# Infini-attention and SwiGLU layers on one core: the memory update's products in four column tiles of two heads, with the instruction order chosen anew

## Chip, cores and metric

The kernel runs on one core of one Trainium2 chip. The metric is the time of one execution in device microseconds, as the median of repeated executions. Five engines work side by side and wait for each other by semaphores: TensorE (PE, with its weight loads shown apart as PEld), VectorE (DVE), ScalarE (ACT), GpSimd (POOL) and SyncE (SP), which issues most DMAs.

## What is computed

The input is one sequence of 2048 tokens with 512 features. Two layers are applied, each an attention block A and a feed-forward block B, each on a layer norm of its input and added back to it. The two layers use the same weights.

```python
def _A_ref(x, wq, wk, wv, wo, beta):       # H = 32 heads of Dh = 16, N = 4 segments of L = 512
    ...                                    # q, k, v: [B, H, N, L, Dh]
    phi = lambda t: jnp.where(t > 0, t + 1.0, jnp.exp(t))
    g = _sigmoid(beta).reshape(1, H, 1, 1)
    for s in range(N):
        logits = einsum('bhqd,bhkd->bhqk', qs, ks) * scale + mask      # causal within the segment
        a_dot = einsum('bhqk,bhkd->bhqd', softmax(logits), vs)
        pq = phi(qs)
        num = einsum('bhld,bhde->bhle', pq, M)
        den = einsum('bhld,bhd->bhl', pq, z)[..., None] + 1e-06
        outs.append(g * (num / den) + (1.0 - g) * a_dot)
        pk = phi(ks)
        M = M + einsum('bhld,bhle->bhde', pk, vs)                      # the memory update
        z = z + einsum('bhld->bhd', pk)
    return o @ wo

def _B_ref(x, w1, w3, w2):                  # 512 -> 1376 -> 512
    return (silu(x @ w1) * (x @ w3)) @ w2
```

Each head keeps a memory M of 16 x 16 and a vector z of 16, which carry from one segment to the next. Only the sums over earlier segments are read, so the update is done after the first three segments of each layer, six times in all.

## The kernel before

The work is cut into eight blocks (two layers of four segments, `g` from 0 to 7). Heads lie in four groups `G` of eight, so that one group's 8 x 16 features fill the 128 partitions.

Per block, `project` makes q and k (features on partitions) and `va` (tokens on partitions, V with a column of ones behind each head's 16, which gives z and the softmax sums along with the products). `attention` goes through 20 units. Each unit has score matmuls (`lg`, line 952, names `R...`), which use row tiles of 32 partitions for four heads at a time; an exp on ScalarE over up to 2048 columns (line 961); and masks on GpSimd (line 974). The four PSUM banks for scores hold one full unit, so a unit's scores wait for the exp of the unit before. In block 0 the units are split in halves. After each group's units follow the products with V (`attend`, line 1003, names `C...`), which use column tiles of 32 columns, their eviction, a DMA transpose (line 1013), the division (`normalise`, lines 1028 to 1041) and another transpose (line 1044). Then come `out_proj`, a layer norm with transposes (lines 692 to 728), and `ffn`, whose g and u matmuls go through a tanh on ScalarE (line 1118) and two multiplications on VectorE (lines 1120 and 1124). The matmuls of projections, feed-forward and the memory all go through the helpers `whole` and `quarters`, so their lines are 388 and 393.

The memory update (`memory_update`): `phi` makes pk from k (exp `px` at line 812, then lines 814 and 816), a DMA transpose (line 825) turns it to tokens on partitions, and for each half `hf` of the groups one call of the op `dacc` multiplies it with `va`. A call makes, for each of two groups and four token tiles, one matmul with 128 weight columns (the group's features) and 136 moving columns (8 heads x 17). Only the 8 diagonal blocks of 16 x 17 of each product are wanted, the other heads' blocks are computed beside them. VectorE adds the product to the sum `macc` (line 844, 272 columns), and multiplies the sum with the 0/1 pattern `bdm` into `mb` (line 846), which clears the unwanted blocks. In the next block `memory_read` multiplies pq with `mb`: `mden` (8 columns, the denominators) and four `mnum` (128 columns), and VectorE divides (`om`, line 882).

The order of all instructions on each engine is chosen when the kernel is built: the class `Sched` places ops one by one by estimated durations, with priorities. `SLACK`, `LOOK`, `C_AGE` and `MARGIN` shape how it picks; `PRIO`, `GATE` and `FINE` shift single groups of ops, by block. An op has a mode: `R` for row tiles, `C` for column tiles, `F` otherwise. Matmuls that may be done either way (`flex`) stand, per pass between two score units, all as four column tiles (`quarters`) when the pass holds an op of mode `C` and all others are flexible, and whole otherwise:

```python
split = any(x.mode == "C" for x in run) and all(x.mode == "C" or x.flex for x in run)
for x in run:
    x.wide = not split
```

An op of mode `C` that became ready less than `C_AGE` ago is put behind all others while the pass is not one of column tiles. `hand_over` adds waits of GpSimd for some ops of VectorE in the first 70 us of the plan.

Of the kernel before, what the change touches and what calls it, by code (L numbers as in the profile page):

```python
# [4 lines left out]
ALU = mybir.AluOpType  # L5
BF16 = mybir.dt.bfloat16
F32 = mybir.dt.float32

P = 128
# [3 lines left out]
NCG = 4  # L13
# [4 lines left out]
LT = 4  # L18
# [18 lines left out]
MARGIN = {"": 300.0, "bnag": 500.0, "bnst": 200.0, "d": 200.0, "dacc": 300.0, "evk": 500.0, "evq": 50.0, "evv": 300.0, "gpr": 800.0, "hmr": 200.0, "lnrs": 200.0, "lnve": 100.0, "macc": 100.0, "mden": 100.0, "mnum": 500.0, "mrec": 1200.0, "norm": 300.0, "oT": 1200.0, "oadd": 100.0, "ph": 500.0, "phexp": 200.0, "phmin": 300.0, "pkT": 3000.0, "q": 200.0, "r": 100.0, "resA": 100.0, "resB": 500.0, "t": 2000.0, "tanh": 50.0}  # L37


class Pool:  # L40
# [373 lines left out]
def o_pe(ns):  # L414
# [4 lines left out]


PRIO = {
    ("bnst", 1): -51.1, ("bnst", 2): 1000, ("d", 0): 301.1, ("evX", 0): 1329.07, ("evk", 2): 1000, ("evv", 1): 599.1,
    ("g", 2): 6366.8, ("g", 4): 6907.74, ("g", 5): 990, ("gp", 0): -603.05, ("gpr", 1): 300, ("k", 2): 49.98,
    ("k", 3): 652.13, ("k", 4): -4638.56, ("k", 6): -2000.08, ("km", 0): 1000, ("mblk", 0): 1000,
    ("mden", 3): 2359.82, ("mrec", 2): -996.7, ("norm", 6): 999.95, ("o", 5): 2080.58, ("phexp", 3): -939.7,
    ("phmin", 1): -9.95, ("phmin", 2): -1651.05, ("phmin", 6): -337.3, ("q", 1): -2343.51, ("q", 6): -4830.46,
    ("r", 5): -1301, ("rdg", 6): 300, ("tanhr", 1): 300, ("u", 0): 394.62, ("u", 6): -310.2, ("v", 1): 40.3,
    ("v", 3): -1300.1,
}
GATE = {  # L430
    ("bnst", 2): -76, ("bnst", 3): 2, ("bnst", 4): -1, ("bnst", 5): 2, ("km", 3): 19, ("km", 4): 16, ("km", 7): 14,
    ("ph", 0): -38, ("phexp", 0): -10, ("q", 1): 3, ("q", 2): 5, ("v", 1): -211, ("v", 2): -2, ("v", 4): 1,
    ("v", 6): 5, ("v", 7): 10,
}
FINE = {
    ("", 0, 8): 1000, ("bnag", 4, 5): 50, ("d0", 4, 6): 1001, ("d1", 3, 1): 1, ("d1", 5, 3): 1351, ("d1", 5, 6): 1299,
    ("d2", 3, 0): 50, ("d3", 1, 6): 0.1, ("d3", 2, 2): 43.3, ("d3", 2, 5): 1.25, ("evX", 0, 2): -1000,
    ("evX", 2, 3): -1000, ("evX", 2, 7): -1000, ("evX", 3, 6): 3, ("evv", 1, 1): 2050, ("exp", 3, 0): 0.05,
# [5 lines left out]
    ("lnve", 1, 0): -1003, ("macc", 5, 1): -50, ("mask", 0, 1): -990, ("mask", 0, 14): -3700, ("mask", 0, 18): -3,  # L444
    ("mask", 5, 20): -301, ("mnum", 1, 2): -0.95, ("mnum", 5, 3): -10, ("mrec", 6, 0): -47, ("norm", 1, 1): -326.19,
    ("norm", 1, 2): -1111.33, ("norm", 1, 3): -902.53, ("norm", 2, 6): -997, ("norm", 3, 3): -10,
    ("norm", 4, 3): -1050, ("norm", 5, 1): 950, ("norm", 6, 7): -3, ("o0", 6, 0): 300.1, ("o0", 7, 0): 300,
# [8 lines left out]
}  # L456


def build(nc, A_x, A_wq, A_wk, A_wv, A_wo, A_beta, B_w1, B_w3, B_w2, out):
# [9 lines left out]
    def sb(name, shape, dt=BF16):  # L469
        return nc.alloc_sbuf_tensor(name, shape, dt)  # L470
# [351 lines left out]
    def memory_update(g, z, pkb):  # L822
        kt = new("W")
        for hf in range(2):
            dmaT(lambda e, hf=hf: e.dma_start_transpose(
                pkt_r[kt.slot][:, 2 * hf:2 * hf + 2, :, :].rearrange("p g i c -> p (g i) c"),
                pk_r[pkb.slot][:, 2 * hf:2 * hf + 2, :].rearrange("p g n -> p (g n)")),
                 reads=[(pkb, hf)], writes=[(kt, hf)], bufs=[pkb, kt], prio=g + 0.1, name="pkT")
        mb = new("mb")
        for hf in range(2):  # L830
            B = new("B")

            def fn(e, mm, hf=hf, B=B):
# [10 lines left out]
            dve(lambda e, B=B, mv=mv: e.tensor_tensor(mv, bank(B)[:, 0:272], mv, ALU.add), 272, True,  # L844
                reads=[(B, 0), ("macc", hf)], writes=[("macc", hf)], bufs=[B], prio=g - 95.0, name="macc")
            dve(lambda e, hf=hf: e.tensor_tensor(mb_r[mb.slot][:, 2 * hf:2 * hf + 2, :, :].rearrange("p a h d -> p a (h d)"),
                                                 macc[:, 2 * hf:2 * hf + 2, :, :].rearrange("p a h d -> p a (h d)"),
                                                 bdm[:].rearrange("p h d -> p (h d)")[:, None, :].to_broadcast([P, 2, 136]), ALU.mult),
                375, reads=[("macc", hf), "bdm"], writes=[(mb, hf)], bufs=[mb], prio=g - 300, name="mblk")
        mstate["mb"] = mb  # L850

# [77 lines left out]
    def attention(s, g, z, oms, parts):  # L929
        z.ot = new("W")  # L930
        cnt = 0
        for pi, part in enumerate(parts):
# [219 lines left out]
    for layer in range(2):  # L1152
        for s in range(NS):
# [8 lines left out]
                gth_op = gate_constants()  # L1162
            z = project(s, g, X, g == 0)
            if s == 0 and layer == 1:
                pool(lambda e: e.memset(macc[:], 0.0), 544, writes=[("macc", 0), ("macc", 1)], prio=g)
            oms = None
            if s > 0:
                pqb = new("W")
# [61 lines left out]
```

## Time and profile before

| | |
|---|---|
| time, median of 3 runs | 486.26 us (486.24 to 486.32) |
| span of the profiled execution | 483.3 us |
| time outside the span, by the median | 2.96 us |
| TensorE, matmuls busy | 469.3 us |
| VectorE busy | 392.0 us |
| ScalarE busy | 392.4 us |
| GpSimd busy | 244.7 us |
| matmuls of `dacc` | 88 whole, 32 in column tiles recorded |

The profile's page names no separate time for the profiled execution. Its span, from the first to the last instruction, stands for it, and the rest to the median lies around it. Busy matmul time includes the latency of each matmul at its end, so a TensorE that is shown as busy may still have room; steps from one start to the next are more reliable. A row of grouped instructions shows line, engine, operation, out<-in, shapes and count, then busy time and mean duration, then the idle time just before them and what ended it. A few per cent of the matmul records can be missing.

### The profile page before, as it was taken

What the parts mean: (1) busy time and instruction counts of PE and PEld (TensorE: products, weight loads), DVE (VectorE), ACT (ScalarE), POOL (GpSimd) and SP (SyncE); (2) the same over time, 40 slices, a digit from 0 to 9 for tenths busy, and PEclk for the clock granted to TensorE, in tenths of its full rate; (3) what the DMA queues carried; (4) which work ended last, traced back from release to release, by engine and by line L of the source; (5) the groups of instructions that cost most, each with busy time, mean ns of one, the idle gap of its engine ahead of it and who ended that gap; (6) DMA issues with size and microseconds to landing.
All of it is one profiled execution on the core that took longest, in us unless ns stands there. A gap on an engine that the chain in (4) does not pass through costs nothing.

```text
span 483.3 us, 13285 instructions
## 1 busy us (share of the span) xinstructions
PE 469.3 (97%) x5619; PEld 223.5 (46%) x5654; DVE 392.0 (81%) x814; ACT 392.4 (81%) x356; POOL 244.7 (51%) x380
## 2 busy tenths in 40 slices
PE   7989999999999999999999999999999999999997
PEld 4543446754444444444444444544444434455544
DVE  5999899988988888779986789876996697578572
ACT  2999999989989987899989999889998799730230
POOL 4777455853546545656565556665473464510000
PEclk9999999999999999999999999999999999999999
DMA  7778367342235622451462324524064322320401
GB/s 257 260 131 147 72 123 88 63 72 55 23 77 84 91 41 41 71 92 37 66 99 56 67 44 78 88 58 63 3 100 72 61 56 56 73 50 14 90 3 45
DMA packets 106522, 37.07 MB, mean 77 GB/s; under 512 B 99200, under 2 KB 104448, under 8 KB 106464
## 3 DMA queue, kind: packets, MB, share of 16 engines
q1 hardware_dynamic: 104016, 31.41, 35.0%
q0 software_dynamic: 1488, 4.03, 4.3%
q8 instruction: 44, 0.72, 0.6%
q10 hardware_dynamic: 960, 0.79, 0.5%
q14 instruction: 14, 0.11, 0.1%
HBM read 8.43 MB, written 2.10 MB: 22 GB/s over the span
## 4 chain that ended last, share of the span: by engine, by line
PE 81%; DVE 7%; ACT 5%; issue 4%; DMA 2%; POOL 0%; SPq 0%; POOLq 0%
PE psall L388 49%; PE psall L393 12%; PE psall L952 11%; PE psall L1003 7%; ACT e L961 3%; DVE W L551 2%; DMA W<-W 1%; DMA W<-xn 1%; PE psall L581 1%; DVE W L816 1%; ACT px L812 1%; DVE xn L710 1%; DVE xs L551 1%; ACT th L1118 0%; DVE x_tok L1056 0%
## 5 line engine op out<-in xcount | busy, mean ns | idle before, releaser
L961 ACT ACTIVATE e<-psall 128x2048 bf16<-128x2048 f32 (+1 forms) x180 | 301.3, 1700 | 29.3 <-PE psall L952 27.6
L974 POOL TENSOR_SCALAR_AFFINE_SELECT e<-e 128x512 bf16<-128x512 bf16 x256 | 164.2, 660 | 164.5 <-ACT e L961 156.9
L388 PE MATMUL psall<-W,w 128*128 128x512 bf16 (+1 forms) x521 | 110.0, 350 | 0.0
L388 PEld LDWEIGHTS psall<-W,w 128*128 128x128 bf16 x521 | 47.0, 98 | 44.9 <-issue 8.1
L1120 DVE SCALAR_TENSOR_TENSOR gp<-th,psall 128x512 bf16<-128x512 bf16 x80 | 53.7, 679 | 15.1 <-ACT th L1118 14.9
L1118 ACT ACTIVATE th<-psall 128x512 bf16<-128x512 f32 x80 | 47.2, 602 | 18.8 <-PE psall L393 17.5
L1124 DVE SCALAR_TENSOR_TENSOR h<-gp,psall 128x512 bf16<-128x512 bf16 x80 | 54.2, 679 | 8.1 <-PE psall L388 7.4
L388 PE MATMUL psall<-w,h 128*128 128x512 bf16 (+1 forms) x218 | 53.8, 380 | 1.4 <-issue 1.0
L393 PE MATMUL psall<-W,w 128*32 128x512 bf16 (+1 forms) x796 | 44.5, 371 | 0.0
L692 DVE BATCH_NORM_STATS2 ln<-x_tok 128x6 f32<-128x512 bf16 x64 | 42.3, 681 | 0.3
L1003 PE MATMUL psall<-e,va 128*32 128x256 bf16 (+3 forms) x1088 | 41.4, 292 | 1.2 <-POOL e L974 1.2
L952 PE MATMUL psall<-W 16*128 16x256 bf16 (+3 forms) x544 | 41.4, 294 | 0.5 <-ACT e L961 0.3
L952 PE MATMUL psall<-W,km 32*128 32x256 bf16 (+3 forms) x544 | 40.8, 291 | 0.3
L551 DVE CAST W<-psall 128x512 bf16<-128x512 f32 x46 | 31.0, 681 | 8.4 <-PE psall L388 7.9
L1143 DVE TENSOR_TENSOR x_tok<-psall,x_tok 128x512 bf16<-128x512 f32 (+1 forms) x33 | 22.1, 670 | 19.4 <-PE psall L393 10.7
L388 PE MATMUL psall<-W,wk 128*128 128x512 bf16 (+1 forms) x137 | 32.9, 356 | 0.7 <-DVE W L551 0.5
L551 DVE CAST xs<-psall 128x512 bf16<-128x512 f32 x38 | 25.6, 682 | 9.6 <-PE psall L1003 9.4
L1003 PEld LDWEIGHTS psall<-e,va 128*32 128x32 bf16 x1088 | 24.6, 96 | 18.0 <-issue 2.8
L388 PEld LDWEIGHTS psall<-w,h 128*128 128x128 bf16 (+1 forms) x233 | 20.9, 98 | 25.9 <-issue 4.8
L952 PEld LDWEIGHTS psall<-W 16*128 16x128 bf16 x544 | 13.1, 91 | 42.0 <-ACT e L961 39.1
L710 DVE TENSOR_SCALAR xn<-x_tok,ln 128x512 bf16<-128x512 bf16 x64 | 29.5, 504 | 3.6 <-POOL ln L701 3.5
L1036 POOL TENSOR_TENSOR og<-xg,rd 128x256 bf16<-128x256 bf16 (+1 forms) x45 | 25.5, 584 | 10.2 <-DVE rd L1030 8.2
(87 smaller groups left out, 589.0 us busy)
## 6 DMA issues: line engine op xcount, KB each, us to landing
w<-in_B_w_dram SPq DMA_DIRECT2D x4, 688.0 KB, 8.1
out_dram<-x_tok SPq DMA_DIRECT2D x15, 128.0 KB, 1.7
km<-W POOLq DMA_DIRECT2D x24, 64.0 KB, 2.7
w<-in_B_w_dram POOLq DMA_DIRECT2D x3, 384.0 KB, 4.1
x_tok<-in_A_x_dram POOLq DMA_DIRECT2D x2, 512.0 KB, 4.7
xg<-xs SPq DMA_TRANSPOSE x36, 3.1
W<-og SPq DMA_TRANSPOSE x36, 2.4
wk<-in_A_wk_dram SPq DMA_DIRECT2D x1, 512.0 KB, 4.4
```

Of the source, the lines that this page charges most:

```text
L388: return e.matmul(out, lhsT, rhs, **k)
L393: o = e.matmul(out[c:c + 32], lhsT[:, c:c + 32], rhs, tile_position=(0, c), **k)
L551: return e.tensor_copy(dst(), src())
L692: dve(lambda e: e.bn_stats(ln_r[st.slot][:, i, 0:6], x_tok[:, tt, :]), 540, reads=[("x", tt)], writes=[(st, 0, i)], bufs=[st], prio=prio, ...
L710: op = S.add([o_dve(512, False, 1.45)], lambda e, i=i, k=k, tt=tt, xn=xn: e.tensor_scalar(xn_r[xn.slot][:, k, :], x_tok[:, tt, :], ln_r[st ...
L952: o = e.matmul(S4[:, sps(pg), c:c + n], kk[32 * pg:32 * pg + r, G, 128 * j:128 * j + 128], q_r[z.q.slot][32 * pg:32 * pg + r, G, 128 * t1 ...
L961: act(lambda e, N=N, ebuf=ebuf, pgs=pgs, sps=sps: e.activation(e_r[ebuf.slot][:, pgs[0]:pgs[-1] + 1, 0:N], S4[:, sps(pgs[0]):sps(pgs[-1]) ...
L974: pool(lambda e, ebuf=ebuf, c=c: e.affine_select(e_r[ebuf.slot][:, :, c:c + 128], e_r[ebuf.slot][:, :, c:c + 128], pattern=[[0, 4], [1, 128]],
L1003: o = e.matmul(bank(X)[32 * pg:32 * pg + 32, base + W - n:base + W], va_r[z.va.slot][:, j, h:h + 32], e_r[eb.slot][:, pg, c:c + n], start= ...
L1118: act(lambda e, NW=NW, B=B, th=th: e.activation(th_r[th.slot][:, 0:NW], bank(B)[:, 0:NW], ACT.Tanh, scale=0.5), NW, reads=[(B, 0)], writes ...
L1120: dve(lambda e, NW=NW, B=B, th=th, gp=gp: e.scalar_tensor_tensor(gp_r[gp.slot][:, 0:NW], th_r[th.slot][:, 0:NW], 1.0, bank(B)[:, 0:NW], AL ...
L1124: dve(lambda e, NW=NW, B=B, gp=gps[fg], h=hs[fg]: e.scalar_tensor_tensor(h_r[h.slot][:, 0:NW], gp_r[gp.slot][:, 0:NW], 0.5, bank(B)[:, 0:N ...
```

## The change

A call of `dacc` makes four matmuls where it made one: each takes 32 weight columns (two heads' features), goes to a column tile of its own, and has as moving columns only those two heads' 34. The sum `macc` keeps 34 columns for each group and not 136: per 32 partitions the two heads' blocks of 17. The multiplication into `mb` reads these 34 columns four times over, once for each place, times the pattern, and still writes all 136 columns of a group. The op is given mode `C` and stands no longer among the flexible ones. All constants of the order are new.

```diff
-SLACK = {"pe": 30.0, "act": 60.0, "dve": 60.0, "pool": 0.0, "sp": 30.0}
-LOOK = {"pe": 90.0, "act": 10.0, "dve": 10.0, "pool": 5.0, "sp": 200.0}
-C_AGE = 3000.0
+SLACK = {"pe": 37.0, "act": 72.0, "dve": 89.0, "pool": 112.0, "sp": 27.0}
+LOOK = {"pe": 91.0, "act": 30.0, "dve": 20.0, "pool": 80.0, "sp": 302.0}
+C_AGE = 6933.0
...
 PRIO = {
...
 GATE = {
...
 FINE = {
...
-    macc = sb("macc", [P, NCG, 8, 17], F32)
+    macc = sb("macc", [P, NCG, 34], F32)
...
-    pool(lambda e: e.memset(macc[:], 0.0), 544, writes=[("macc", 0), ("macc", 1)], prio=CP + 3)
+    pool(lambda e: e.memset(macc[:], 0.0), 136, writes=[("macc", 0), ("macc", 1)], prio=CP + 3)
...
-            def fn(e, mm, hf=hf, B=B):
+            def fn(e, hf=hf, B=B):
                 o = None
                 for a in range(2):
                     G = 2 * hf + a
                     for i in range(LT):
-                        o = mm(e, bank(B)[:, 136 * a:136 * a + 136], pkt_r[kt.slot][:, G, i, :],
-                                     vheads(va_r[z.va.slot], i, 8 * G, 8)[:, :, 0:17], start=(i == 0), stop=(i == LT - 1))
+                        for c in range(4):
+                            o = e.matmul(bank(B)[32 * c:32 * c + 32, 34 * a:34 * a + 34], pkt_r[kt.slot][:, G, i, 32 * c:32 * c + 32],
+                                         vheads(va_r[z.va.slot], i, 8 * G + 2 * c, 2)[:, :, 0:17], start=(i == 0), stop=(i == LT - 1),
+                                         tile_position=(0, 32 * c))
                 return o
-            pe(fn, 8 * 65, reads=[(kt, hf)] + [(z.va, i) for i in range(LT)], writes=[(B, 0)],
+            pe(fn, 8 * 30, mode="C", reads=[(kt, hf)] + [(z.va, i) for i in range(LT)], writes=[(B, 0)],
                bufs=[B, kt, z.va], hold=[mb], prio=g + 0.3 - 900, name="dacc")
-            mv = macc[:, 2 * hf:2 * hf + 2, :, :].rearrange("p a h d -> p (a h d)")
-            dve(lambda e, B=B, mv=mv: e.tensor_tensor(mv, bank(B)[:, 0:272], mv, ALU.add), 272, True,
+            mv = macc[:, 2 * hf:2 * hf + 2, :].rearrange("p a h -> p (a h)")
+            dve(lambda e, B=B, mv=mv: e.tensor_tensor(mv, bank(B)[:, 0:68], mv, ALU.add), 68, True,
                 reads=[(B, 0), ("macc", hf)], writes=[("macc", hf)], bufs=[B], prio=g - 95.0, name="macc")
-            dve(lambda e, hf=hf: e.tensor_tensor(mb_r[mb.slot][:, 2 * hf:2 * hf + 2, :, :].rearrange("p a h d -> p a (h d)"),
-                                                 macc[:, 2 * hf:2 * hf + 2, :, :].rearrange("p a h d -> p a (h d)"),
-                                                 bdm[:].rearrange("p h d -> p (h d)")[:, None, :].to_broadcast([P, 2, 136]), ALU.mult),
+            dve(lambda e, hf=hf: e.tensor_tensor(mb_r[mb.slot][:, 2 * hf:2 * hf + 2, :, :].rearrange("p a (c h) d -> p a c (h d)", h=2),
+                                                 macc[:, 2 * hf:2 * hf + 2, :][:, :, None, :].to_broadcast([P, 2, 4, 34]),
+                                                 bdm[:].rearrange("p (c h) d -> p c (h d)", h=2)[:, None, :, :].to_broadcast([P, 2, 4, 34]), ALU.mult),
                 375, reads=[("macc", hf), "bdm"], writes=[(mb, hf)], bufs=[mb], prio=g - 300, name="mblk")
...
-    SPLIT = (0,)
+    SPLIT = 20
...
-                groups = [(0, 1), (2, 3)] if g in SPLIT else [(0, 1, 2, 3)]
+                groups = [(0, 1), (2, 3)] if g == 0 and cnt < SPLIT else [(0, 1, 2, 3)]
```

`PRIO`, `GATE`, `FINE` and `MARGIN` have other entries throughout, and the memset of `macc` between the layers shrinks as the first one does. Counted in the built order, `dacc` has twelve calls of 32 matmuls where it had eleven of 8 and one of 32; score units come in 179 passes where there were 178; and 28 evictions of `va` stand on VectorE and 4 on ScalarE, where there were 23 and 9.

More of the change, by code (lines that the diff above doesn't have):

```diff
@@ L33 @@
 R_SLACK = 0.0
-SLACK = {"pe": 30.0, "act": 60.0, "dve": 60.0, "pool": 0.0, "sp": 30.0}
-LOOK = {"pe": 90.0, "act": 10.0, "dve": 10.0, "pool": 5.0, "sp": 200.0}
-C_AGE = 3000.0
-MARGIN = {"": 300.0, "bnag": 500.0, "bnst": 200.0, "d": 200.0, "dacc": 300.0, "evk": 500.0, "evq": 50.0, "evv": 300.0, "gpr": 800.0, "hmr": 200.0, "lnrs": 200.0, "lnve": 100.0, "macc": 100.0, "mden": 100.0, "mnum": 500.0, "mrec": 1200.0, "norm": 300.0, "oT": 1200.0, "oadd": 100.0, "ph": 500.0, "phexp": 200.0, "phmin": 300.0, "pkT": 3000.0, "q": 200.0, "r": 100.0, "resA": 100.0, "resB": 500.0, "t": 2000.0, "tanh": 50.0}
+SLACK = {"pe": 37.0, "act": 72.0, "dve": 89.0, "pool": 112.0, "sp": 27.0}
+LOOK = {"pe": 91.0, "act": 30.0, "dve": 20.0, "pool": 80.0, "sp": 302.0}
+C_AGE = 6933.0
+MARGIN = {"": 50.0, "XT": 1200.0, "bnag": 500.0, "bnst": 100.0, "d": 200.0, "dacc": 300.0, "evX": 100.0, "evk": 500.0, "evq": 100.0, "evv": 300.0, "exp": 50.0, "g": 50.0, "gpr": 200.0, "hT": 100.0, "hmr": 500.0, "k": 50.0, "ldbeta": 500.0, "ldw": 500.0, "ldwk": 50.0, "ldwo": 3000.0, "ldwq": 300.0, "ldwv": 800.0, "ldx": 50.0, "lnrs": 800.0, "lnve": 300.0, "macc": 50.0, "mask": 50.0, "mblk": 500.0, "mde": 200.0, "mden": 200.0, "mnum": 500.0, "mrec": 1200.0, "norm": 300.0, "oT": 3000.0, "oadd": 500.0, "om": 50.0, "ph": 500.0, "phexp": 200.0, "phmin": 300.0, "pkT": 3000.0, "q": 200.0, "r": 300.0, "resA": 100.0, "resB": 500.0, "stx": 300.0, "t": 2000.0, "tanh": 50.0, "u": 50.0, "warm": 100.0, "xT": 800.0, "xt": 200.0}
 class Pool:
@@ L421 @@
 PRIO = {
[L422 to L426, printed above, removed]
@@ L427 @@
-    ("r", 5): -1301, ("rdg", 6): 300, ("tanhr", 1): 300, ("u", 0): 394.62, ("u", 6): -310.2, ("v", 1): 40.3,
-    ("v", 3): -1300.1,
+    ("bnag", 2): 598.5, ("bnag", 3): 1321.3, ("bnag", 4): -3404.9, ("bnag", 5): -2272, ("bnst", 3): 125.9, ("d", 1):
+    3258.4, ("d", 3): 2319.2, ("evk", 3): 1034.2, ("evq", 2): 2243.6, ("evv", 1): 463.6, ("evv", 2): -181.7, ("exp",
+    5): -133.8, ("g", 2): 8591.1, ("g", 4): 9710.64, ("gp", 2): -2081.1, ("hmr", 7): 1313.8, ("k", 2): 36.38, ("k",
+    4): -5667.56, ("k", 6): -5229.18, ("km", 1): 3839.8, ("lnrs", 5): 1479, ("lnve", 0): 1277, ("lnve", 4): -692.5,
@@ new lines @@
+    ("mask", 2): 135.9, ("mask", 3): 356.6, ("mden", 3): 1473.72, ("mden", 6): -676.3, ("mnum", 3): 406.9, ("mnum",
+    6): -5341.9, ("mrec", 3): -474, ("norm", 5): 2198.8, ("o", 4): -1099.5, ("o", 5): 2352.98, ("ph", 0): -122.8,
+    ("ph", 1): -2832.4, ("phexp", 0): -3794.5, ("phexp", 3): -3111.5, ("phexp", 5): 3154.1, ("phmin", 2): -6822.85,
+    ("phmin", 3): -1266.3, ("phmin", 6): 3338.8, ("q", 1): -1403.51, ("q", 6): -8143.16, ("r", 1): -122.2, ("r", 5):
+    -3416.4, ("rd", 2): 13.4, ("rdg", 5): 657.7, ("t", 2): 1662.4, ("u", 0): -161.4, ("u", 2): -0.8, ("u", 3):
@@ L429 @@
+    -1109, ("u", 4): -2518.4, ("v", 3): -2015.7,
 }
 GATE = {
-    ("bnst", 2): -76, ("bnst", 3): 2, ("bnst", 4): -1, ("bnst", 5): 2, ("km", 3): 19, ("km", 4): 16, ("km", 7): 14,
-    ("ph", 0): -38, ("phexp", 0): -10, ("q", 1): 3, ("q", 2): 5, ("v", 1): -211, ("v", 2): -2, ("v", 4): 1,
-    ("v", 6): 5, ("v", 7): 10,
+    ("bnst", 2): -1, ("bnst", 3): 3, ("bnst", 4): -3, ("k", 4): -17, ("km", 3): 16, ("km", 4): 17, ("km", 7): 17,
+    ("ph", 0): -101, ("phexp", 0): -24, ("q", 1): 4, ("v", 1): -201, ("v", 3): 1, ("v", 4): 2, ("v", 6): 10, ("v",
@@ L434 @@
+    7): 4,
 }
 FINE = {
-    ("", 0, 8): 1000, ("bnag", 4, 5): 50, ("d0", 4, 6): 1001, ("d1", 3, 1): 1, ("d1", 5, 3): 1351, ("d1", 5, 6): 1299,
-    ("d2", 3, 0): 50, ("d3", 1, 6): 0.1, ("d3", 2, 2): 43.3, ("d3", 2, 5): 1.25, ("evX", 0, 2): -1000,
-    ("evX", 2, 3): -1000, ("evX", 2, 7): -1000, ("evX", 3, 6): 3, ("evv", 1, 1): 2050, ("exp", 3, 0): 0.05,
[5 rows of a table removed]
-    ("lnve", 1, 0): -1003, ("macc", 5, 1): -50, ("mask", 0, 1): -990, ("mask", 0, 14): -3700, ("mask", 0, 18): -3,
-    ("mask", 5, 20): -301, ("mnum", 1, 2): -0.95, ("mnum", 5, 3): -10, ("mrec", 6, 0): -47, ("norm", 1, 1): -326.19,
@@ L1164, in build @@
             if s == 0 and layer == 1:
-                pool(lambda e: e.memset(macc[:], 0.0), 544, writes=[("macc", 0), ("macc", 1)], prio=g)
+                pool(lambda e: e.memset(macc[:], 0.0), 136, writes=[("macc", 0), ("macc", 1)], prio=g)
             oms = None
```

3 lines of the change are left out of this document (1 added, 2 removed), and 24 rows, old and new, of the table FINE.

## The prediction

> **What bounds the kernel now.** I read the page first: the busy shares and the chain that ended last.
>
> ```profile
> span 483.3 us, 13285 instructions
> PE 469.3 (97%) x5619; PEld 223.5 (46%) x5654; DVE 392.0 (81%) x814; ACT 392.4 (81%) x356; POOL 244.7 (51%) x380
> PE 81%; DVE 7%; ACT 5%; issue 4%; DMA 2%; POOL 0%; SPq 0%; POOLq 0%
> ```
>
> TensorE is busy nearly throughout and carries 81% of the chain. But a busy matmul row contains pipeline latency, so I asked for windows next (columns: elapsed, then busy time of PE, PEld, DVE, ACT, POOL).
>
> ```profile
> 33.00:57.00 24.00, 23.77 (x306) 10.93 (x310) 21.07 (x56) 23.98 (x30) 16.24 (x28) 1.00 0.72 116
> 57.00:82.00 25.00, 23.95 (x274) 12.62 (x269) 23.93 (x52) 24.66 (x22) 13.62 (x23) 1.00 0.62 103
> 82.00:108.50 26.50, 26.24 (x351) 16.95 (x355) 24.10 (x54) 24.39 (x22) 17.87 (x26) 1.00 0.49 74
> 108.50:419.00 310.50, 306.99 (x3176) 137.00 (x3205) 255.38 (x522) 282.13 (x237) 168.90 (x256) 1.00 0.37 64
> ```
>
> Two regimes. From 33 to 82 us ScalarE is full (23.98 of 24.00, 24.66 of 25.00): there a shorter matmul is worth nothing, a shorter ScalarE stretch everything. From 82 to 419 us TensorE is the tighter engine; between 108.5 and 419 it idles 310.50 - 306.99 = 3.5 us, and that is all that a better order could win there. The clock is 1.00 throughout.
>
> How a unit of attention works is in the timeline of PE (start, duration).
>
> ```profile
> 356.33 0.40 PE L952 MATMUL psall<-W 16*128 16x512 bf16 x4
> 356.66 2.55 PE L388 MATMUL psall<-W,w 128*128 128x512 bf16 x11
> 359.14 0.40 PE L952 MATMUL psall<-W 16*128 16x384 bf16 x8
> ```
>
> Score matmuls (L952) stand 2.81 us apart (359.14 - 356.33), with eleven 512-column matmuls between: (2.55 - 0.38) / 10 = 0.217 us each, 0.38 being the last one's own duration by the same group's mean (380 ns, quoted below). So the pass between two scores is plain work on TensorE, plus about 0.1 us at each change between score and other matmuls. Reducing work inside such passes shortens the kernel one for one, as long as ScalarE's exp, 1.88 us a unit, is ready.
>
> ```profile
> L961 ACT ACTIVATE e<-psall 128x2048 bf16<-128x2048 f32 x140 | 263.2, 1880 | 28.1 <-PE psall L952 26.4
> ```
>
> **The tail** was read separately, because work behind the last score may be only filler.
>
> ```profile
> 418.84 0.40 PE L952 MATMUL psall<-W,km 32*128 32x384 bf16 x8
> 422.63 1.26 PE L1003 MATMUL psall<-e,va 128*32 128x512 bf16 x32
> 423.72 13.34 PE L393 MATMUL psall<-W,w 128*32 128x512 bf16 x244
> 436.88 3.63 PE L393 MATMUL psall<-wo,W 128*32 128x512 bf16 x64
> 452.52 0.84 PE L393 MATMUL psall<-w,W 128*32 128x192 bf16 x32 [0.97 <-DMA W<-xn]
> 424.66 1.24 SPq L1013 DMA_TRANSPOSE xg<-xs  x1
> 432.56 1.19 SPq L1044 DMA_TRANSPOSE W<-og  x1
> 446.08 2.61 SPq L728 DMA_TRANSPOSE W<-xn  x2
> 447.43 5.05 DMA W<-xn
> 452.52 27.68 PE psall L393 x571
> ```
>
> After the last scores (418.84) come filler, the last product with V (422.63), more filler, the output projection (436.88), filler, and at 452.52 the last feed-forward, 27.68 us. That last one waited 0.97 us for the transposed `xn`. The path there is transposes and vector work (424.66, 432.56, 446.08), so the 33.68 us from 418.84 to 452.52 hang on that path, and filler removed there only becomes waiting.
>
> **The change, part by part.**
>
> *The products.* One row per form: 136 columns on the whole array, 136 columns in four column tiles (one call of before ran so already), and the denominator's 8-column matmuls as the nearest tiny ones.
>
> ```profile
> L388 PE MATMUL psall<-W,w 128*128 128x512 bf16 x376 | 91.3, 380 | 0.0
> L388 PE MATMUL psall<-va,W 128*128 128x136 bf16 x88 | 7.1, 226 | 0.4 <-DMA W<-W 0.2 <-DVE om L882 0.2
> 33.04 0.66 PE L388 MATMUL psall<-va,W 128*128 128x136 bf16 x8
> 44.17 0.66 PE L388 MATMUL psall<-va,W 128*128 128x136 bf16 x8
> 68.21 0.66 PE L388 MATMUL psall<-va,W 128*128 128x136 bf16 x8
> 71.50 0.66 PE L388 MATMUL psall<-va,W 128*128 128x136 bf16 x8 [0.20 <-DVE om L882]
> 83.40 0.66 PE L388 MATMUL psall<-va,W 128*128 128x136 bf16 x8
> 86.92 0.67 PE L393 MATMUL psall<-va,W 128*32 128x136 bf16 x32
> L388 PE MATMUL psall<-mb,W 128*128 128x8 bf16 x96 | 3.5, 176 | 0.0
> 78.44 0.58 PE L388 MATMUL psall<-mb,W 128*128 128x8 bf16 x16
> ```
>
> A whole call has step (0.66 - 0.226) / 7 = 62 ns, so it takes 8 x 62 = 0.50 us. In tiles the eight groups of four have the same step, (0.67 - 0.226) / 7 = 63 ns: four tiles stream together. With 34 columns a group streams a quarter. Bounds of its step: a quarter of 62, 15 ns, and 62, no gain at all. The nearest row for a step not set by columns is the 8-column one: (0.58 - 0.176) / 15 = 27 ns. I take 27: a call costs 0.22 us, 0.28 less (bounds 0.37 and 0). Of twelve calls, four stand early (33.04, 44.17, 68.21, 71.50), where ScalarE is full, and earn nothing. Eight earn: **-2.24 us** (bounds -3.0, 0).
>
> [...]
>
> *What waits on the products.* Counted in the two orders with the steps above, the next denominator (`mden`) stands at least 12 us of TensorE work behind the products that it reads (before: 6). The two vector steps between cost
>
> ```profile
> L844 DVE TENSOR_TENSOR macc<-psall,macc 128x272 f32<-128x272 f32 x12 | 5.1, 430 | 0.2
> L846 DVE TENSOR_TENSOR mb<-macc,bdm 128x272 bf16<-128x272 f32 x12 | 6.1, 511 | 0.1
> ```
>
> The sum shrinks from 272 to 68 columns (bounds: 0 to 0.35 us less each; I take 0.2, off the path); the spreading multiply keeps its 272 results. So that a product now waits for a column pass costs nothing: these 12 us cover it. The smaller clearing of `macc` on GpSimd is off the path as well. `SPLIT` changes nothing: all 20 units of the first block stay split.
>
> *The order, TensorE.* Counted in the two orders: before, 125 four-tile groups of 512 columns stand behind the last scores outside the projection and the last feed-forward; after, 116. Nine groups are pulled ahead: 9 x 0.217 = **+1.94 us** on the passes where TensorE bounds. The tail gains little:
>
> ```profile
> W<-og SPq DMA_TRANSPOSE x36, 2.4
> ```
>
> From the last V product to the projection stand 57 groups, 12.4 us, where before had 61, 13.2; the path between needs 11.2 to 12.4 (423.72 to a transpose issued at 432.56, with 2.4 of landing, from the issue or from its end at 433.75), so it just fits. Two more groups stand ahead of the V product. Two groups net: **-0.4 us** (bounds -1 to +0.6).
>
> *The order, ScalarE.*
>
> ```profile
> L812 ACT ACTIVATE px<-W 128x1024 bf16<-128x1024 bf16 x24 | 25.8, 1075 | 0.0
> L550 ACT ACTIVATE va<-psall 128x512 bf16<-128x512 f32 x9 | 5.4, 602 | 0.0
> ```
>
> Within the first 40 exps one `px` goes and one eviction comes: 1.08 - 0.60, **-0.47 us**, at full value. Within the next 20 stands one `px` more, +1.08; only the first half of that block is full, so **+0.5 us** (bounds 0, +1.08). Net five evictions of `va` move to VectorE, all behind that block, where both have room.
>
> *The waits.* Of the 3.5 us in which TensorE idles I take a fifth as gone, **-0.7 us**, a choice: slightly less work is asked of VectorE before the reads of `mb`. Bounds -2.5, +2.5.
>
> Sum: -2.24 + 1.94 - 0.4 - 0.47 + 0.5 - 0.7 = -1.37 us. The page gives no other time for its execution than the span, 483.3; the median of the runs is 486.26, and the 2.96 us around the span stay. So 486.26 - 1.37 = **484.9 us**. About 0.2%, 0.97 us, is what a measurement of this kernel can tell from no change.
>
> **The rivals.** *The waits go*: all the idle time that can go, -2.5 for -0.7, gives 483.1. For it: 3.5 us are there. Against: they are many small ones.
>
> *ScalarE holds the second block to its end* (108.5): the calls at 83.40 and 86.92 earn nothing either, six are left, -1.68, and `px` counts in full: -1.68 + 1.94 - 0.4 - 0.47 + 1.08 = +0.47, 486.7. For it: 24.39 of 26.50. Against: TensorE 26.24.
>
> *The calls do not get shorter* (slower): the step of a group stays near 62 ns since four weight loads and four matmuls must be handed over for it. Then the pulled work is not paid: 1.94 - 0.4 - 0.47 + 1.08 = +2.15, 488.4. Its far end is 27 ns for each matmul in series, 0.86 for 0.50 us, 8 x 0.36 more, 491.3. [...] It decides from a step of about 45 ns, where eight calls save 1.1 us. For it: no group shorter than 128 columns is in the trace in tiles. [...]
>
> That the change doesn't do what it says is out: the built order has twelve calls of 32 matmuls with 34 columns.
>
> **How the numbers follow.** Chances: the forecast 0.40, waits gone 0.13, ScalarE 0.20, calls not shorter 0.27, of which 0.05 for the far end. Faster 0.53, same 0.20, slower 0.27. The range leaves out that far end and as much of the others: from 482.4 (the waits gone and the step at 15 ns, 483.1 - 0.7) to 489.4 (488.4 and the tail at its bound). The forecast alone: 484.0 to 485.3.
>
> **What would show it.** Right: `va,W` rows of 34 columns with a call of about 0.4 us from first start to last end (0.2 and the last matmul's own 0.2), `macc` near 0.2 us, the last scores about 1 us earlier, a wait of 2 to 3 us for `xn` ahead of the last feed-forward, ScalarE as full as before to 82 us. Wrong: a call of 0.6 us or more; the last scores not earlier although the calls are short, which would mean waits of the new order; or no wait ahead of the last feed-forward, which would mean that the tail hangs on work after all.

## The result and the profile after

The changed kernel takes 483.3 us (median of 6 runs, 481.6 to 483.83), the kernel before 486.25 us beside it (6 runs). The ratio is 0.9944, with a 95% interval of 0.9927 to 0.9961: 2.7 us faster (2.95 us between the two medians), where 1.4 us were forecast. The runs of either kernel lie on two levels some 1.5 us apart, so only ratios of runs on one chip are compared below.

The page of the changed kernel (span, busy shares, chain), then its groups by shape (mean ns behind the comma).

```profile
span 479.9 us, 14227 instructions
...
PE 467.6 (97%) x6090; PEld 222.1 (46%) x6122; DVE 390.6 (81%) x816; ACT 389.9 (81%) x351; POOL 245.4 (51%) x383
...
PE 79%; ACT 13%; DVE 6%; issue 1%; DMA 1%
```

```profile
L843 DVE TENSOR_TENSOR mb<-macc,bdm 128x272 bf16<-128x272 f32 x12 | 5.9, 494 | 0.0
...
L834 PE MATMUL psall<-va,W 128*32 128x34 bf16 x384 | 4.8, 180 | 0.0
...
L841 DVE TENSOR_TENSOR macc<-psall,macc 128x68 f32<-128x68 f32 x12 | 2.7, 221 | 0.5 <-PE psall L834 0.5
```

The calls are what was forecast: 34 columns, the sum `macc` near 0.2 us, `mb` hardly shorter. The windows show ScalarE still full to 82 us, as forecast, and TensorE after it as full as before.

```profile
33.00:57.00 24.00, 23.95 (x369) 10.30 (x369) 21.02 (x58) 24.00 (x29) 12.92 (x23) 1.00 0.58 106
57.00:82.00 25.00, 23.59 (x342) 12.55 (x341) 23.10 (x50) 24.84 (x24) 16.70 (x29) 1.00 0.61 119
82.00:108.50 26.50, 26.16 (x472) 17.74 (x473) 23.92 (x54) 24.57 (x22) 17.19 (x26) 1.00 0.36 55
```

The surprise is in the tail. The timeline of PE and the last lines of the chain:

```profile
417.47 0.40 PE L949 MATMUL psall<-W,km 32*128 32x384 bf16 x8
...
421.73 1.27 PE L1000 MATMUL psall<-e,va 128*32 128x512 bf16 x32
...
435.13 3.63 PE L393 MATMUL psall<-wo,W 128*32 128x512 bf16 x64
...
448.73 0.84 PE L393 MATMUL psall<-w,W 128*32 128x192 bf16 x32 [0.36 <-DMA W<-xn]
```

```profile
445.56 3.12 DMA W<-xn
448.73 27.68 PE psall L393 x569
```

From the last scores to the last feed-forward it is 448.73 - 417.47 = 31.26 us, where before had 33.68. A wait of 2 to 3 us for `xn` was forecast there; it is 0.36 us. The landing of the last transposed `xn` took 3.12 us, before 5.05.

The whole span in stretches, from the starts in the timelines of ScalarE (first exp, 61st exp) and PE (last scores, last feed-forward), in us. Second traces of both kernels and the three experiments that matter most stand beside them. The tail goes from the last scores to the last feed-forward, the rest from there to the end. (In the last two kernels the first matmuls of the last feed-forward run on from the group ahead without a gap, in one row, and its start is taken from the single matmuls.)

| kernel | to first exp | to 61st exp | to last scores | tail | rest | span |
|---|---|---|---|---|---|---|
| before | 12.04 | 96.49 | 310.31 | 33.68 | 30.8 | 483.3 |
| before, second trace | 13.01 | 96.64 | 310.39 | 33.58 | 30.8 | 484.4 |
| after | 11.73 | 95.54 | 310.20 | 31.26 | 31.2 | 479.9 |
| after, second trace | 11.20 | 95.57 | 310.78 | 31.27 | 31.1 | 479.9 |
| new order, old products | 11.58 | 96.81 | 312.73 | 31.28 | 31.1 | 483.5 |
| old order, new products | 12.33 | 96.70 | 311.99 | 32.54 | 30.8 | 484.4 |
| the same, 30 instructions less | 11.53 | 96.79 | 309.24 | 32.54 | 30.8 | 480.9 |

### The profile page after: what moved, and what is told of

Read it like the earlier page. It is cut to its first block, busy times and chain, and to the rows that moved or that the text cites. A ratio compares the mean times of both kernels' runs of the same rounds, so it can differ in the third digit from the quotient of the medians.

```text
span 479.9 us, 14227 instructions
## 1 busy us (share of the span) xinstructions
PE 467.6 (97%) x6090; PEld 222.1 (46%) x6122; DVE 390.6 (81%) x816; ACT 389.9 (81%) x351; POOL 245.4 (51%) x383
## 4 chain that ended last, share of the span: by engine, by line
PE 79%; ACT 13%; DVE 6%; issue 1%; DMA 1%
PE psall L388 45%; PE psall L393 19%; ACT e L958 10%; PE psall L949 9%; PE psall L1000 6%; ACT px L807 1%; PE psall L576 1%; DVE x_tok L1053 1%; DMA W<-xn 1%; DVE om L879 1%; DVE W L811 1%; DVE xs L546 1%; DVE W L809 1%; PE psall L834 1%; DVE gp L1117 1%
## 5 line engine op out<-in xcount | busy, mean ns | idle before, releaser
L388 PE MATMUL psall<-W,w 128*128 128x512 bf16 (+1 forms) x494 | 103.3, 351 | 0.6 <-DVE W L546 0.3
L388 PEld LDWEIGHTS psall<-W,w 128*128 128x128 bf16 x494 | 44.9, 98 | 43.2 <-issue 7.9
L388 PE MATMUL psall<-w,h 128*128 128x512 bf16 (+1 forms) x203 | 49.1, 380 | 1.1 <-issue 0.6
L393 PE MATMUL psall<-W,w 128*32 128x512 bf16 (+1 forms) x904 | 49.9, 368 | 0.1
L546 DVE CAST W<-psall 128x512 bf16<-128x512 f32 x46 | 31.2, 681 | 5.2 <-PE psall L388 5.1
L393 PEld LDWEIGHTS psall<-W,w 128*32 128x32 bf16 x904 | 23.3, 97 | 20.5 <-issue 0.9
L388 PE MATMUL psall<-W,wk 128*128 128x512 bf16 (+1 forms) x131 | 31.7, 355 | 0.5 <-DVE W L546 0.5
L393 PE MATMUL psall<-w,h 128*32 128x512 bf16 (+3 forms) x588 | 32.0, 363 | 0.0
```

Of the source, the lines that this page charges most:

```text
L388: return e.matmul(out, lhsT, rhs, **k)
L393: o = e.matmul(out[c:c + 32], lhsT[:, c:c + 32], rhs, tile_position=(0, c), **k)
L546: return e.tensor_copy(dst(), src())
```

## Experiments: the two halves of the change

**Products alone and order alone.** The first kernel keeps the order of before op for op and takes the new products; the second keeps the new order and takes the old ones.

```diff
 first: before, with memory_update's products and macc of the change, and
-            split = any(x.mode == "C" for x in run) and all(x.mode == "C" or x.flex for x in run)
+            split = any(x.mode == "C" or x.name == "dacc" for x in run) and all(x.mode == "C" or x.flex for x in run)
 second: after, with memory_update's products and macc of before, and
-            split = any(x.mode == "C" for x in run) and all(x.mode == "C" or x.flex for x in run)
+            split = any(x.mode == "C" and x.name != "dacc" for x in run) and all(x.mode == "C" or x.flex for x in run)
```

> The kernel before, with its order of every engine kept op for op, and only the products changed: twelve calls of 32 tiled matmuls with 34 columns, the sum of 34 columns for each group; passes that hold a call go in column tiles. Theory A (the products earn where TensorE bounds, the order gives part of it back): nothing is pulled ahead here, so the last scores come some 1.9 to 2.2 us earlier than 418.84 us in the profile (eight calls of 0.28 us); the tail behind them, all filler, keeps its length or grows by what it waits; the time goes to about 484 to 484.5 us. Theory B (the gain was made by the new order alone, above all in the first block, and the products earn next to nothing): last scores at 418.4 to 419.1, time 486.3. The va,W rows read about 0.4 us a call in both.

> The changed kernel, with its order of every engine kept op for op, and only the products and the sum put back to 136 columns on the whole array (passes that were column-tiled for them alone go whole). Theory A: it loses what eight calls earned, 2.2 us: last scores at about 419.7 instead of 417.47 us, time about 485.5. Theory B: last scores stay at 417.4 to 417.8, time 483.3 to 483.7. In both, the first exp of the second block's units (the 21st) stays near 31.8 us against 33.0 before, since the first block has no memory product on its path.

Measured: products alone 485.97 us, ratio 1.0012 (1.0001 to 1.0022); order alone 485.21 us, ratio 0.9999 (0.9989 to 1.0010). Each half alone earns nothing, both together 2.7 us. Theory B falls: the order alone is not the gain. Theory A falls as well in its first half. The price of a call is not in question. Timeline of PE, new order with old products, then the changed kernel, the same place:

```profile
240.35 0.67 PE L388 MATMUL psall<-va,W 128*128 128x136 bf16 x8
240.86 1.89 PE L388 MATMUL psall<-W,w 128*128 128x512 bf16 x8
```

```profile
237.59 0.38 PE L834 MATMUL psall<-va,W 128*32 128x34 bf16 x32
237.81 1.92 PE L393 MATMUL psall<-W,w 128*32 128x512 bf16 x32
```

240.86 - 240.35 = 0.51 us for a call before, 0.22 now. So with the old order the saving must have turned into waits, and its timeline shows two that before does not have. Products alone, then before at the same two places:

```profile
157.74 1.46 PE L388 MATMUL psall<-W,wk 128*128 128x512 bf16 x6 [1.22 <-DVE h L1126]
...
363.63 0.51 PE L393 MATMUL psall<-w,W 128*32 128x192 bf16 x16 [0.94 <-DVE gp L1095]
```

```profile
155.87 1.46 PE L388 MATMUL psall<-W,wk 128*128 128x512 bf16 x6
...
360.78 1.18 PE L393 MATMUL psall<-w,W 128*32 128x192 bf16 x48
```

The names of the releasers mislead here; the matmuls that waited read a transposed `xn`. The first was issued at 152.35 and landed at 157.65, after 5.29 us (3.19 in before); the other at 357.56 landed after 5.94 us (4.46). The chain's landing of 5.05 us in the tail of before is a third of the kind. What makes a transpose land late?

## Experiments: where TensorE's instructions are fetched

The page counts a DMA queue of its own kind. Before, then after:

```profile
q8 instruction: 44, 0.72, 0.6%
```

```profile
q8 instruction: 48, 0.79, 0.7%
```

Packets of 16 KB (0.72 MB in 44), about 1 us each (median 1.04 us in both traces), one in about 256 TensorE instructions (5,619 matmuls and 5,654 weight loads over 44 packets in before: 256; 6,090 and 6,122 over 48 in after: 254). That the queue feeds TensorE is read from these counts and from where the packets fall: on average 254 TensorE instructions lie between the starts of two, in before (203 to 325) as in after (117 to 337), while the time between them goes from 4.1 to 16.4 us. The second trace of before has 44 packets for 11,308 TensorE instructions, the one of before with 64 matmuls more 45 for 11,436. Shorter matmuls in greater number move every later fetch to another place in the work: the 30th starts at 352.89 us in before, at 304.85 us in after.

**First try.** Before with 64 tiny matmuls more, after with 20 more (the edit is shortened here).

```diff
                     def flip(e, xn=xn, k=k, tb=tb, B=B):       # in the second block
+                        for _ in range(16):                    # 5 in the changed kernel
+                            e.matmul(bank(B)[:, 400:408], xn_r[xn.slot][:, k, 0:128], xn_r[xn.slot][:, k, 0:8], start=True, stop=True)
```

> The kernel before with 64 tiny matmuls more (8 columns, into unused columns of a bank, 16 in each of four transposes of the second block, where ScalarE bounds; 128 TensorE instructions with their weight loads). In the trace of before, TensorE's instructions are fetched in packets of 16 KB about every 256 of its instructions, and one such fetch at 450.4 us lies on the landing of the transposed xn, which then took 5.05 us instead of 3.12 in the changed kernel. The 128 extra instructions move every later fetch about half a period, 3.5 us, away from that place. Theory C (the fetch delays the landing): the transposed xn lands in about 3.1 us, the tail from last scores to last feed-forward falls from 33.68 to about 31.7 us, and the time falls by 1.5 to 2 us, to about 484.5, although work was added. Theory D (the landing is late for the store that was issued ahead of it on the same queue, or for another cause that is not the fetch): landing 5 us as before, tail 33.7, time 486.3 to 486.8.

> The changed kernel with 20 tiny matmuls more (5 in each of the same four transposes; 40 TensorE instructions), which moves the fetch of TensorE's instructions at 448.58 us to about 447.5, onto the landing of the transposed xn (issued 444.28, landed 448.68). Theory C: the landing takes 1.5 to 2 us longer, the tail grows from 31.26 to about 33 us, the time rises from 483.3 to about 485. Theory D: landing 3.1 us, tail 31.3, time 483.3 to 483.6.

Measured: before with 64 more 487.32 us, ratio 1.0042 (1.0026 to 1.0058); after with 20 more 481.82 us, ratio 0.9925 (0.9911 to 0.9940). Neither theory's time came. In the first the last `xn` landed after 3.07 us, as theory C has it, and the tail fell to 32.5 us with no wait for `xn`. But the tiny matmuls weren't free: 64 at the 27 ns of the prediction's row are 1.7 us, and the time from the first to the 61st exp grew from 96.5 and 96.6 us to 97.7. A transpose of pk issued at 233.98 us landed late instead, after 7.17 us (5.54 and 5.49 in the two traces of before), with 1.9 us of waiting. Right behind that wait the granted clock of this execution was 0.50, from 242.8 to 246.2 us, so its stretch from the 61st exp to the last scores is not compared. In the second kernel the fetch did not come where it was sent: it started at 449.08 us, only 0.15 us ahead of the landing at 449.23, which took 3.16 us.

**The same shift in three kernels.** To move the fetches without work on the path, warm-up matmuls at the start are replaced by tiny ones (shortened here).

```diff
         def spin(e, B=new("B")):      # seven ops of two matmuls each
-            for _ in range(2):
-                o = e.matmul(bank(B), xs_r[0][:, 0, 0:128], xs_r[0][:, 0, :], start=True, stop=True)
+            o = e.matmul(bank(B), xs_r[0][:, 0, 0:128], xs_r[0][:, 0, :], start=True, stop=True)
+            for _ in range(9):        # in three of the ops; 11 in all seven for the last kernel
+                o = e.matmul(bank(B)[:, 0:8], xs_r[0][:, 0, 0:128], xs_r[0][:, 0, 0:8], start=True, stop=True)
```

> The kernel of the first experiment (products in tiles, order of before) with nothing changed but its warm-up at the start: 3 of the 14 warm-up matmuls of 512 columns are replaced by 9 matmuls of 8 columns each, so that 48 more TensorE instructions (with their weight loads) stand ahead of all work, in about the same time. Every fetch of TensorE's instructions (16 KB, one in about 256 instructions) then falls 48 instructions earlier in the work. Theory H: a fetch asked for from about 1.3 us ahead of a DMA transpose's issue to 1.0 us behind it makes that transpose land about 1 us later, and where TensorE waits for it the kernel loses that. Moved by 48 in the trace of the first experiment, the fetches hit four further transposes that TensorE waits for (issued at 151.1, 234.3, 305.1 and 327.0 us) beside two that are hit already: 2 to 4 us slower than the first experiment, which was 486.0 against 485.3 for before, so 488 to 490. Theory G (the old order's waits are its own, fetches don't matter): no change, 486.0.

> The changed kernel with the same edit of the warm-up, 48 TensorE instructions more. By theory H, moved by 48 its fetches hit no transpose that TensorE waits for and that was not hit: at most 0.3 us slower, ratio to before 0.994 to 0.995. Theory G: no change. This is the control for the edit itself: if this run is slower by a microsecond or more, the warm-up edit has a price of its own and the other three are read against it.

> The kernel before with the same edit of the warm-up, 48 TensorE instructions more. Theory H: the fetches now fall on two transposes that TensorE waits for and that were free (issued at 226.5 and 447.4 us): 0.7 to 1.7 us slower, ratio 1.0015 to 1.0035. Theory G: no change, ratio 1.000.

> The changed kernel with 7 of the 14 warm-up matmuls replaced by 11 of 8 columns each: 140 TensorE instructions more ahead of all work. Theory H: the fetches hit the last block's transposes that TensorE waits for (issued at 431.0, 444.3 and 445.6 us) and one in the middle: about 3 us slower, so that nothing is left of the gain over before (ratio 0.999 to 1.002). Then the order that was chosen anew is good for the place of its fetches as much as for its work. Theory G: no change, ratio 0.994.

Measured, as ratios to before: products alone with 48 more 1.0036 (1.0023 to 1.0049); the changed kernel with 48 more 0.9957 (0.9941 to 0.9973); before with 48 more 0.9994 (0.9984 to 1.0003); the changed kernel with 140 more 1.0006 (0.9994 to 1.0019).

The first lost 0.24% or 1.2 us more, less than forecast. All four places forecast did land later: 151.34 us after 5.38, 234.25 after 7.20, 306.81 after 4.92, 329.10 after 4.69, where products alone had 4.16, 5.44, 3.27 and 3.16. One that was late there, at 357.6, no longer was (4.40 us for 5.94). Timeline of PE at the second of them:

```profile
238.46 1.25 PE L393 MATMUL psall<-W,w 128*32 128x512 bf16 x20
241.58 0.38 PE L845 MATMUL psall<-va,W 128*32 128x34 bf16 x32 [1.87 <-DMA W<-W]
```

The control, 0.9957, lies a little above the forecast of 0.994 to 0.995, and its interval holds both that and the changed kernel's 0.9944. Before with 48 more is a miss of theory H: no loss came where 0.7 to 1.7 us were forecast. The transpose at 227.07 landed late as forecast, and one at 433.12 that was not forecast (3.57 and 3.93 us, 2.40 and 2.42 before), but TensorE did not wait for either: the step to the projection behind the first is 0.49 us, as in the second trace of before. The other place that was forecast, the last `xn`, had been late in before already and landed a little sooner (4.42 us for 5.05). The parts moved all the same: 52.66 us from the 41st to the 61st exp, for 51.66 and 51.86 in before, and a tail of 33.06 for 33.68 and 33.58.

With 140 more the whole gain is gone, 3.0 us as forecast, but not all of it for that reason: the first exp started at 13.68 us against 11.20 and 11.73, so some 2 us are the price of that warm-up. The rest is in the tail, 32.59 us for 31.26, with waits for the last two `xn`. A wait in the middle is hardly seen at the last scores, which come 310.76 us after the 61st exp (310.20 and 310.78 in the two traces of the changed kernel). The transpose forecast at 431.0 was not late (2.45 us).

```profile
141.88 0.82 PE L388 MATMUL psall<-w,W 128*128 128x192 bf16 x8 [1.02 <-DMA W<-xn]
...
450.81 0.84 PE L393 MATMUL psall<-w,W 128*32 128x192 bf16 x32 [0.59 <-DMA W<-xn]
...
452.66 0.84 PE L393 MATMUL psall<-w,W 128*32 128x192 bf16 x32 [1.00 <-DMA W<-xn]
```

**Thirty instructions less, and second traces.** The most telling edit adds nothing: in the old order with the new products, the other matmuls of two early passes that hold a call are left whole, where ScalarE is full.

```diff
+            calls += any(x.name == "dacc" for x in run)
-            split = any(x.mode == "C" or x.name == "dacc" for x in run) and all(x.mode == "C" or x.flex for x in run)
+            split = any(x.mode == "C" or (x.name == "dacc" and calls > 2) for x in run) and all(x.mode == "C" or x.flex for x in run)
```

> The kernel of the first experiment (products in tiles, order of before), in which the other matmuls of the two passes of the first block that hold a call stay whole: 12 quarter matmuls less in number each way, 30 TensorE instructions less, in the part of the kernel where ScalarE is full. Theory H (fetches of TensorE's instructions that fall beside a DMA transpose delay it): all later fetches come 30 instructions later in the work and, moved so in the trace of the first experiment, leave the transpose issued at 152.4 us, whose lateness cost 1.2 us there, and the one at 118.4: time 0.5 to 1.2 us below the first experiment, ratio to before 0.999 to 1.000. Theory G (the old order's waits are its own): as the first experiment, 1.001 to 1.002.

> The changed kernel once more, for a second trace and a time on the chip of the others. Theory H: its fetches keep clear of the transposes that TensorE waits for, as in the first trace: last scores at 417.4 to 417.8 us, the tail 31.3 us from the last scores to the last feed-forward, ratio to before 0.9935 to 0.995. If the tail were longer than 32 us here, the landing of the last transposes would be chance from one execution to the next and not the place of the fetch.

> The kernel before once more, for a second trace. In the first one the transposed xn of the last block landed after 5.05 us and the last feed-forward waited 0.97 us for it, which makes a tail of 33.68 us; with the same order and other fetch places the tail was 32.5 us twice and 33.1 us once. If the late landing belongs to this program's fetches, it is 4.5 us or more again and the tail 33 us or more; if it was that one execution's chance, the landing is 3.1 to 3.3 us and the tail 32.5. Idle time of TensorE between 108.5 and 416 us is below 1 us if all records of matmuls are there.

> The changed kernel with 20 tiny matmuls in the second block (the fourth experiment, ratio 0.9925 there) beside the changed kernel on one chip. If it is the better version its ratio lies 0.001 to 0.002 below that of the changed kernel; if the two differed by chance, within 0.0008 of it.

Measured: products alone with 30 instructions less 483.65 us, ratio 0.9963 (0.9951 to 0.9975), 0.49% or 2.4 us below the same kernel with them. That is twice what was forecast, since the second wait went too and not only the first. Up to the 41st exp both take 44.73 us from the first; from there to the last scores the difference, 2.7 us, lies in the two stretches of twenty exps that hold those waits (1.68 and 1.12 us). The DMA of the window about the first of them, with the instructions and without:

```profile
q8 instruction: 1, 0.02, 1.6%
...
W<-xn SPq DMA_TRANSPOSE x2, 4.7
```

```profile
q14 instruction: 1, 0.01, 0.3%
...
W<-xn SPq DMA_TRANSPOSE x2, 4.0
```

The second window has no q8 row: the fetch has left it, the second of the two transposes lands after 3.75 us and not 5.29, and TensorE goes on at once:

```profile
154.47 1.04 PE L390 MATMUL psall<-W,w 128*128 128x512 bf16 x4
155.34 1.46 PE L390 MATMUL psall<-W,wk 128*128 128x512 bf16 x6
```

The changed kernel again gave 0.9940 (0.9919 to 0.9960) with a tail of 31.27 us; before again had the late landing (4.95 us) and a tail of 33.58. So these belong to the program, not to one execution. The changed kernel with 20 tiny matmuls gave 0.9927 (0.9909 to 0.9945): lower than the changed kernel both times, but the intervals overlap, so whether it is better by some 0.7 us stays open.

Over 13 traces (all but that of the changed kernel with 48 more, whose granted clock was 0.975), I sorted the DMA transposes by whether a fetch started from 0.5 us ahead of their issue to 2.0 us behind it. These edges were set with the traces at hand; theory H had named others, for the moment at which a fetch is asked for, which no trace shows. Medians from issue to landing, in us (counts in brackets):

| | no fetch | fetch |
|---|---|---|
| `xn` | 3.21 (293) | 4.08 (69) |
| `og` | 2.44 (362) | 3.51 (103) |
| `xs` to `xg` | 3.07 (344) | 3.86 (118) |
| `hr` | 2.44 (89) | 3.87 (27) |
| pk | 3.71 (119) | 4.28 (34) |

The late transposes at 152.35 (fetch 2.04 us behind the issue), 233.98 and 234.25 (3.94 and 3.81 us) lie outside these edges. A sharper comparison sets each transpose beside itself: its undisturbed landing is its median over the kernels of the same order in which no fetch starts between 1 us ahead of its issue and 0.3 us behind its landing (at least three of them). A fetch that starts up to 3 us behind that undisturbed landing changes nothing (median 0.0 us, 346 cases). One that starts 0.5 to 1.5 us ahead of it makes the transpose 1.5 us late (65 cases), one 2 to 3 us ahead 0.7 us (84 cases). In the last half microsecond ahead of it a good part of the 57 cases are not late at all, and the others by some 1.7 us. So what counts is a fetch that starts while the transpose is under way. The transpose at 234 us takes 5.44 to 5.54 us undisturbed, and the fetches at 3.94 and 3.81 us fell within it.

The late `xn` in the tail of before lies outside this window, with the fetch 3.0 us behind the issue. The packets of the trace show it at 450.45 to 451.37 us, store packets of 1 KB ahead of it, beside it and behind it (from 449.89 us on), and the last two of the 4-byte packets ahead of the landing (452.47) at 452.08 and 452.43. In the changed kernel the fetch has the same distance (448.58), but the last of these packets had come at 448.59, and the landing at 448.68. In four other kernels of the old order the same transpose took 3.07 to 3.15 us, with the same stores issued around it, so the stores alone (theory D) don't make it late; but in one of the four a fetch 2.4 us behind its issue did no harm either. That the fetch is the cause in the tail of before too is likely by this; no run shows it by itself.

## Why the prediction came out as it did

The sign and the range held; the time was 1.6 us too long.

**The calls** (27 ns for a group of four, 0.22 us): right. In the trace of after the groups start 25 ns apart (median; 27 on average). The rival in which calls don't get shorter is out, and so is its far end, 27 ns for each of 32 matmuls in series: its 0.86 us a call are 0.22. The trace of before spoke against that end already: in its one call in tiles (86.92 us) the 32 matmuls start within 0.67 - 0.226 = 0.44 us, 14 ns apart.

**Eight of twelve calls earn**: wrong, and differently in the two orders. In the old order with the fetches out of the way, the time up to the 61st exp is no shorter (96.79 against 96.49 and 96.64), as in the rival where ScalarE holds the second block: six calls earn, 1.1 us from there to the last scores, where six times 0.28 are 1.7; why not all of it stays open. In the new order all of them earn: from old products to new the two stretches lose 1.2 and 2.0 to 2.5 us, about twelve times 0.28, and the ratios differ by 0.0055, 2.7 us. Part of that may again be fetches in other places; why the early calls earn there was not tried.

**Nine groups pulled ahead**, +1.94 (9 x 0.217 is 1.95): about right. With old products the new order takes 2.34 to 2.42 us more from the 61st exp to the last scores. But TensorE idles 2.2 us of that trace between 108.5 and 416 us, where before idles 0.9 (below), so the agreement is not that of the nine groups alone.

**The tail**, -0.4: the step that failed. It said that the 33.68 us hang on a fixed path of transposes and that filler taken out there becomes waiting. Four kernels with the tail of before and no late landing had 32.5 us and no wait: the tail hung on its work, plus 1.1 us of one late landing, which I had read as the path's own length. In the new order it is 31.26 to 31.30 us in every trace without a late landing, 1.28 less, two thirds of the nine groups; the remainder is the wait of 0.36 us and its surroundings. In all -2.4 instead of -0.4.

**The waits**, -0.7 of 3.5 us: the idle time wasn't there. A line of the waits of the first trace of before (for what, total, times, longest), then a window of it, then the same window of the second trace:

```profile
PE psall L388 <- issue: 2.1, 13, 0.2
```

```profile
108.50:416.00 307.50, 303.99 (x3158) 135.88 (x3183) 253.36 (x518) 279.79 (x236) 167.31 (x253) 1.00 0.37 64
```

```profile
108.50:416.00 307.50, 306.62 (x3190) 136.12 (x3188) 254.34 (x519) 279.57 (x237) 167.37 (x253) 1.00 0.36 63
```

The thirteen waits of 0.2 us for "issue" are, by the counts, matmuls whose records are missing: the first trace has 5,619 matmuls and 5,654 weight loads, the second 5,654 of both, and no such waits. With all records TensorE idles 0.9 us between 108.5 and 416. The rival "the waits go" came close to the measured time (483.1), but not for its reason: in the second trace of the changed kernel, also complete, it is 1.9 us.

**ScalarE's first 60 exps**, -0.47 + 0.5: 96.49 to 96.81 us for the order alone, near the forecast, but by luck, since both halves were larger. Up to the 41st exp the order alone takes 43.56 us, where the two traces of before have 44.83 and 44.78: -1.2 to -1.3, of which 0.8 to 0.9 come within the first twenty, where `px` and evictions of `va` are as many as before and the prediction put no term. From there to the 61st it takes 53.25 for 51.66 and 51.86: +1.4 to 1.6, about the full price of the one `px` more (1.08) and of one more eviction of `va` (0.60) that the prediction did not count there. Not forecast at all: the warm-up starts at 1.26 us where before had 2.66, since VectorE clears its input first (at 0.93 us, in before at 2.33), and the first exp comes at 11.2 to 11.7 us in five traces with the new order and at 12.0 to 13.0 in the two of before; one kernel with the old order had 11.53, so this start scatters and its share is not settled.

**Outside the span** stood 2.96 us. The changed kernel's runs show 1.7 to 1.9, each by its own span: the profiled execution lay below the median.

So the sum was near the truth by errors that offset each other: less from waits, more from the tail, two halves of ScalarE's part, an earlier first exp that it didn't have, and a rest that grew by 0.3 to 0.4 us, also with old products. Some 1.1 us of the gain are before's own late landing, which the old order loses too when its fetches move. Where the fetches fall is worth 2 to 3 us in this kernel, as much as the change itself.

## What to carry to other kernels

Before a wait for a transposed tile is taken as the length of a path, compare the landings of the same transfer in all blocks: one that lands a microsecond or two later than they do, as the last `xn` of before here (5.05 us, where the median without a fetch is 3.21), may have been held up by something that an edit elsewhere moves. When a kernel whose engine runs thousands of instructions is changed in their number, measure two or three versions that differ only by a harmless shift of the instructions, before the gain or loss is put down to the edit. And count matmul records against weight loads before short idle times are added up as room.

## What the hardware showed that was not expected

TensorE's instructions come by DMA in packets of 16 KB while the kernel runs (44 in before, 48 in after), and a transpose beside such a packet lands 0.6 to 1.4 us later (medians above), 1.5 us later where the packet starts 0.5 to 1.5 us ahead of the undisturbed landing. Thirty instructions less, far from the place where it shows, made a kernel 2.4 us faster. Column tiles side by side start nearly as one: groups of four 34-column matmuls start 25 ns apart, and the four of a group 4 ns apart (medians of the trace of after).
